# A planned mLSTM and mixture-of-experts kernel: its order found in rounds forward and backward, chunk 0's low halves from SBUF

## The chip, the cores and the metric

One core of a Trainium2 chip. The metric is the device time of the whole kernel in microseconds (us); the time before is the median of three runs.

## What is computed

Three layers, one after the other, all inputs in HBM.

An mLSTM over 4 batches, 8 heads, 768 steps, head width 40, with exponential gates and a running maximum m:

```python
m_new = np.maximum(f_gate[:, :, t] + m, i_gate[:, :, t])
C = f_stab[..., None, None] * C + i_stab[..., None, None] * np.einsum('bhd,bhe->bhde', vt, kt)
n = f_stab[..., None] * n + i_stab[..., None] * kt
denom = np.maximum(np.abs(nq), 1.0)                      # nq = n . q
y[:, :, t] = sigmoid(o_gate) * (C @ q) / denom
```

Its output, 3072 tokens of 320, goes through a dense layer, `h = x @ w_in` (320 x 2048), `g = h * sigmoid(h)`, `x = g @ w_out` (2048 x 320), and then through eight experts: each token goes to the one with the largest gate logit, `gate * relu(x @ w1[e]) @ w2[e]` with 1024 hidden columns. `w_in` and `w_out` come as float64, all else as float32.

## The kernel before, in words

The kernel multiplies in float16 with a high and a low part for each operand: a value is scaled, rounded to its high half, and the low half is the difference. So every product is three (or eight, with 320 = 128 + 128 + 64 rows) matmuls, and every value that feeds one needs a copy (the high half, ScalarE) and a subtraction (the low half, VectorE or GpSimd).

The mLSTM is done in 6 chunks of 128 steps for each of 4 batches: 24 units of 128 tokens (`unit(t)`, L568). Units 0 to 3 are chunk 0. A unit loads k, q, v and the output gate, splits them, turns K and Q (by TensorE for t < 3, by a transposing DMA on SP's queue from t = 3 on, L554 to L566), multiplies K by Q for the scores (L661), gates them (L663), takes high and low half (L667, L669), multiplies by V (L687 to L689), divides by the denominator (`denom`, L695 to L700: copy, absolute value by negation and maximum, maximum with 1 and scaling, reciprocal), takes halves of y and turns it into `xt`. Other than in the last chunk it also updates the batch's state (L724 to L749).

`l1(t, g)` (L902) multiplies tile t by a quarter of w_in (32 matmuls, L921), applies the tanh form of the gate (L923, L927) and takes halves (L930, L933). For t >= 4 and odd g the gated value lies in SBUF and GpSimd takes the low half; else it stays in PSUM and VectorE takes it, since GpSimd works from SBUF here. `l2(t, g)` (L940) multiplies by w_out (L953 to L955). Every four tiles `route` picks the experts and scatters the rows.

The float64 weights are narrowed to float32 by three integer instructions on VectorE (`narrow`, L760): L769 shifts the high word, L772 joins the sign, L775 joins the low word. For w_out (`conv_out`, L833) the middle value goes through `cvo_b`, 2560 bytes of PSUM that fill bank 3 and reach into bank 4. Bank 3 and bank 4 also hold the second layer's sums, in turns. Each converted block of w_out is turned by TensorE through one bank (`wt`, bank 2; L859, L860), copied (L862) and folded with the expert gate's weights (L872).

From the first expert on, 28 slots of 128 rows each (`slot`, L1139) multiply rows by an expert's weights; the weights come through two, later three staging buffers (`load_e`, L1076) and are split by ScalarE and VectorE (L1100 to L1115).

What sets the order: nothing is issued where it stands. Each `op(...)` adds a step to a plan with its engine (or two engines to choose from), a reckoned time, its dependencies and a `rank`, and, for loads, a time before which it may not start (`after`). `Plan.order` (L158) simulates the engines once: at each turn the engine that can start first takes the ready step with the lowest rank. The steps are then issued in the order of the simulated start times, each engine's queue in that order. The ranks come from the tile's position and from the table `RK` (L28). A step marked `port` is kept apart from GpSimd's steps in the simulation. The reckoned times are constants and lines such as

```python
def dve(n):
    return (n + 151) / 0.96
def pool2(n):
    return 100 + 2.25 * n
```

Of the kernel before, what the change touches and what calls it, by code (L numbers as in the profile page):

```python
# [27 lines left out]
RK = dict(  # L28
    tiles=20.71, win=4.19, dwin=3.47, wout=36.32, dwout=1.2, u0=-11.64, u1=12.12, u2=43.76, u3=-70.67,
    lead1=31.42, lead=30.5, l1c=-9.11, l2c=59.64, l2=21.72, gates=35.48, load=15.59, state=26.07, route=20.7,  # L30
)
# [7 lines left out]
def act(n):  # L39
    return 186 + 0.833 * n  # L40
# [6 lines left out]
def dve(n):  # L47
    return (n + 151) / 0.96
# [65 lines left out]
class Plan:  # L114
# [3 lines left out]


    HOP = 120  # L120
    DEEP = 5000
# [35 lines left out]

    def order(self):  # L158
        n = len(self.ops)
        need = [len(o[2]) for o in self.ops]  # L160
        after = [[] for _ in range(n)]
        for i, o in enumerate(self.ops):
            for d in o[2]:
                after[d].append(i)
        at = [max(0.0, o[6]) for o in self.ops]
        engines = ["PE", "ACT", "DVE", "POOL", "SP"]
        free = {e: 0.0 for e in engines}
        wait = {e: [] for e in engines}
        ready = {e: [] for e in engines}
        taken = [None] * n  # L170
        bus = port = begun = 0.0
        out = []

        def offer(i):
            for e in self.ops[i][0]:
                heapq.heappush(wait[e], (at[i], i))

        for i in range(n):
            if need[i] == 0:
                offer(i)  # L180
        while len(out) < n:
            best = None
            for e in engines:
                while ready[e] and taken[ready[e][0][1]]:
                    heapq.heappop(ready[e])
                while wait[e] and taken[wait[e][0][1]]:
                    heapq.heappop(wait[e])
                if ready[e]:
                    t = free[e]
                elif wait[e]:  # L190
                    t = max(free[e], wait[e][0][0])
                else:
                    continue
                if best is None or t < best[0]:
                    best = (t, e)
            t, e = best
            while wait[e] and wait[e][0][0] <= t:
                i = heapq.heappop(wait[e])[1]
                if not taken[i]:
                    heapq.heappush(ready[e], (self.ops[i][3], i))  # L200
# [21 lines left out]
            for j in after[i]:  # L222
# [4 lines left out]
        out.sort(key=lambda x: x[0])  # L227
        self.out = out
        return out

    def emit(self, engines):
# [6 lines left out]
def mlstm_moe_kernel(ctx, tc, q, k, v, ig, fg, og, w_in, w_out, w_gate, w1, w2, out):  # L238
# [20 lines left out]
    def op(*args, **kw):  # L259
        plan[0].op(*args, **kw)  # L260
# [8 lines left out]
    PS = Region(psp, "PS", 16384)  # L269
    groups = dict(l0=[0, 1], l1=[0, 1, 2], l2=[(4, 128), (3, 0)], at=[5, 6, 7], gt=[2], wt=[2], pg=[(2, 480)])  # L270
    turn = dict.fromkeys(groups, 0)
# [296 lines left out]
    def unit(t):  # L568
# [86 lines left out]
        for g in range(2):  # L655
            ps, kk = bank("at", 128, 4, CH)

            def scores(g=g, ps=ps):
                for j in range(4):
                    h = 4 * g + j  # L660
                    pe.matmul(ps[:, j, :], kT.ap[0:120, h, :], qT.ap[0:120, h, :], start=True, stop=True)  # L661
            op("PE", 4 * 60, scores, R=[kT, qT], W=[kk], rank=p + 6 + g)
            op("DVE", dve(512), lambda g=g, ps=ps: ve.scalar_tensor_tensor(  # L663
                out=ps, in0=ps, scalar=1.0 / SQ, in1=lam[g].ap, op0=ALU.mult, op1=ALU.mult
            ), R=[lam[g]], W=[kk], rank=p + 6 + g)
            P2 = P2_b[g]
            op("ACT", act(512), lambda P2=P2, ps=ps: ac.copy(out=P2.ap[:, 0], in_=ps),  # L667
               R=[kk], W=[P2], rank=p + 7 + g)
            op("DVE", dve(512), lambda P2=P2, ps=ps: ve.tensor_tensor(  # L669
                out=P2.ap[:, 1], in0=ps, in1=P2.ap[:, 0], op=ALU.subtract  # L670
            ), R=[kk], W=[P2], rank=p + 7 + g)
        if c > 0:
# [8 lines left out]
            ), R=[ki, "E"], W=[hb], rank=p + 8)  # L681
        pv, kv = bank("at", 128, H, D1)

# [11 lines left out]
        def denom():  # L695
            nq = pv[:, :, D:D1]
            ve.tensor_copy(out=den, in_=nq)
            ve.scalar_tensor_tensor(out=den, in0=den, scalar=-1.0, in1=nq, op0=ALU.mult, op1=ALU.max)
            ve.tensor_scalar(out=den, in0=den, scalar1=SQ * SQ, scalar2=2.0 / SY, op0=ALU.max, op1=ALU.mult)
            ve.reciprocal(out=den, in_=den)  # L700
        op("DVE", 640, denom, R=[kv], W=[kd], rank=p + 11)
        y = pv[:, :, 0:D]
# [54 lines left out]
    cv_b = [PS.cut([128, 512], F32, at=2048 * i) for i in (3, 4)]  # L757
    cvo_b = PS.cut([128, 640], F32, at=2048 * 3)

    def narrow(T, X, mid, z, n, rank):  # L760

        if not wide:
# [13 lines left out]
            out=o, in0=lo, scalar=29, in1=m, op0=ALU.logical_shift_right, op1=ALU.bitwise_or  # L776
        ), R=[T], W=[X, mid], rank=rank)

# [54 lines left out]
    def conv_out(f0):  # L833
# [7 lines left out]
        ), W=[T], rank=rk - 16, lag=2300, move=2100)  # L841
        narrow(T, X, cvo_b, X, 2 * DM, rk)
        pair = wo_b[f0:f0 + 2]
# [58 lines left out]
    def l1(t, g):  # L902
# [8 lines left out]
        for half in range(2):  # L911
# [12 lines left out]
           R=[kk], W=[th], rank=rk)  # L924
        pool_ = g in BY_POOL and t >= B
        z, kz = (th.ap, th) if pool_ else (ps, kk)
        op("DVE", dve(512), lambda: ve.scalar_tensor_tensor(  # L927
            out=z, in0=th.ap, scalar=1.0, in1=ps, op0=ALU.add, op1=ALU.mult
        ), R=[kk, th], W=[kz], rank=rk)
        op("ACT", act(512), lambda: ac.copy(out=G.ap[:, 0], in_=z), R=[kz], W=[G], rank=rk + 2)  # L930
        name, ns = ("POOL", pool2(512)) if pool_ else ("DVE", dve(512))
        m = po if pool_ else ve
        op(name, ns, lambda: m.tensor_tensor(out=G.ap[:, 1], in0=z, in1=G.ap[:, 0], op=ALU.subtract),  # L933
           R=[kz], W=[G], rank=rk + 2)

# [490 lines left out]
```

## Time and profile before

| | us |
|---|---|
| median of 3 runs (lowest to highest) | 691.66 (689.37 to 691.77) |
| the profiled execution, its time | 690.1 |
| its span, first to last instruction | 688.1 |
| busy: TensorE / VectorE / ScalarE / GpSimd | 624.6 / 530.8 / 412.9 / 237.2 |
| mean granted TensorE clock | 0.944 |
| read from and written to HBM | 71.64 MB, 11.78 MB |

In the rows PE is TensorE's matmuls, PEld its weight loads, DVE VectorE, ACT ScalarE, POOL GpSimd, SP the sync engine; SPq and the like are their queues. L921 is line 921 of the kernel before. Names after a line are the memory regions: PS is PSUM, A, W, X, RO and SG are regions of SBUF. Matmuls overlap each other, so a matmul's own duration is longer than the step from one to the next.

### The profile page before, as it was taken

To read this page: it belongs to the slowest core of one execution; us is meant where nothing else is said; L and a number is where in the kernel's file an instruction comes from. 1 tells how busy PE (TensorE), PEld (TensorE's weight loads), DVE (VectorE), ACT (ScalarE), POOL (GpSimd) and SP (SyncE) were. 2 spreads that over 40 slices of the span, in tenths; PEclk is the share of its full clock that TensorE was granted. 3 is DMA by queue.
4 is the path that set the end of the run, shared out by engine and by line. 5 is a ranking of instruction groups with operands and counts; after the bars stand their busy time and mean duration, and the time that the engine had idled before them with its cause. 6 is when DMAs were issued, how large, how long until landed. Compare 5 with 4: busy or idle time off the path is not lost.

```text
span 688.1 us, 21335 instructions
## 1 busy us (share of the span) xinstructions
PE 624.6 (91%) x8494; PEld 529.9 (77%) x8494; DVE 530.8 (77%) x1114; ACT 412.9 (60%) x832; POOL 237.2 (34%) x385
## 2 busy tenths in 40 slices
PE   4628779999999999999999999999979999979993
PEld 3517448898788888888888888887868888768882
DVE  6898678788998899998989989856848666756531
ACT  5754558768768787877777787544325444534320
POOL 3214113315455564538442532412302222313221
PEclk9667679999999999999999999999989999999997
DMA  8971864869978968867994975452479788867700
GB/s 191 233 162 25 190 153 95 211 148 210 197 171 144 169 137 157 159 138 163 147 152 88 187 131 122 124 109 84 126 170 234 222 222 202 218 183 186 165 8 25
DMA packets 254454, 105.96 MB, mean 154 GB/s; under 512 B 193381, under 2 KB 247976, under 8 KB 254344
## 3 DMA queue, kind: packets, MB, share of 16 engines
q1 hardware_dynamic: 251464, 95.82, 66.6%
q0 software_dynamic: 2880, 8.68, 3.5%
q8 instruction: 68, 1.11, 0.7%
q14 instruction: 42, 0.34, 0.2%
HBM read 71.64 MB, written 11.78 MB: 121 GB/s over the span
## 4 chain that ended last, share of the span: by engine, by line
PE 70%; DVE 12%; DMA 7%; ACT 3%; SPq 3%; issue 2%; POOL 0%; POOLq 0%; ACTq 0%; DVEq 0%
PE PS L921 25%; PE PS L953 8%; PE PS L954 8%; PE PS L955 8%; PE PS L1159 6%; DMA SG<-in_moe_w_dram 5%; PE PS L1172 2%; PE PS L1173 2%; PE PS L1174 2%; DMA X<-in_moe_w_dram 2%; PE PS L661 2%; DVE W L1163 1%; DVE A L1104 1%; DVE A L1115 1%; ACT A L1100 1%
## 5 line engine op out<-in xcount | busy, mean ns | idle before, releaser
L921 PE MATMUL PS<-A,A 128*128 128x128 f16 x3072 | 194.4, 221 | 3.0 <-ACT A L566 1.8
L921 PEld LDWEIGHTS <-A 128*128 128x128 f16 x3072 | 180.4, 99 | 8.5 <-issue 2.3
L1159 PE MATMUL PS<-W,A 128*128 128x128 f16 x1792 | 119.2, 222 | 10.5 <-DVE W L1163 10.5
L1159 PEld LDWEIGHTS <-A 128*128 128x128 f16 x1792 | 110.8, 99 | 19.3 <-issue 11.5
L955 PE MATMUL PS<-A,A 128*128 128x328 f16 x344 | 105.5, 307 | 0.0
L953 PE MATMUL PS<-A,A 128*128 128x328 f16 x344 | 105.4, 307 | 0.0
L954 PE MATMUL PS<-A,A 128*128 128x328 f16 x344 | 105.4, 306 | 0.0
L923 ACT ACTIVATE A<-PS 128x512 f32<-128x512 f32 x96 | 57.2, 596 | 54.0 <-PE PS L921 52.8
L1189 POOL DMA_INDIRECT out_dram<-W,sid x28 | 33.5, 1197 | 145.1 <-DVE W L1163 76.9
L933 POOL TENSOR_TENSOR A<-A 128x512 f16<-128x512 f32 x40 | 48.1, 1201 | 80.7 <-ACT A L930 75.9
L1174 PE MATMUL PS<-A,W 128*128 128x320 f16 x224 | 67.5, 301 | 0.9 <-DVE W L1163 0.9
L1172 PE MATMUL PS<-A,W 128*128 128x320 f16 x224 | 67.8, 303 | 0.0
L1173 PE MATMUL PS<-A,W 128*128 128x320 f16 x224 | 67.6, 302 | 0.0
L1163 DVE SCALAR_TENSOR_TENSOR W<-PS,W 128x512 f16<-128x512 f32 x56 | 38.0, 685 | 26.6 <-ACT W L1161 26.3
L616 ACT ACTIVATE A<-A,bias_t 128x128 f32<-128x128 f32 x160 | 58.0, 397 | 0.2 <-POOL A L594 0.2
L1161 ACT ACTIVATE W<-PS 128x512 f16<-128x512 f32 x56 | 32.4, 587 | 42.6 <-PE PS L1159 42.5
L927 DVE SCALAR_TENSOR_TENSOR PS<-A,PS 128x512 f32<-128x512 f32 x56 | 38.5, 688 | 15.3 <-ACT A L923 15.0
L1100 ACT ACTIVATE A<-SG 128x768 f16<-128x768 f32 x34 | 28.6, 841 | 33.9 <-DMA SG<-in_moe_w_dram 33.9
L955 PEld LDWEIGHTS <-A 128*128 128x128 f16 x344 | 34.0, 99 | 15.1 <-issue 0.3
L1104 DVE SCALAR_TENSOR_TENSOR A<-SG,A 128x512 f16<-128x512 f32 x34 | 25.5, 751 | 25.5 <-ACT A L1100 25.3
L953 PEld LDWEIGHTS <-A 128*128 128x128 f16 x344 | 33.9, 99 | 12.0
L954 PEld LDWEIGHTS <-A 128*128 128x128 f16 x344 | 34.0, 99 | 11.7
(247 smaller groups left out, 1353.6 us busy)
## 6 DMA issues: line engine op xcount, KB each, us to landing
SG<-in_moe_w_dram SPq DMA_DIRECT2D x34, 320.0 KB
A<-lam_d SPq DMA_DIRECT2D x40, 256.0 KB
SG<-in_moe_w_dram SPq DMA_DIRECT2D x34, 256.0 KB
A<-in_moe_w_out_dram SPq DMA_DIRECT2D x8, 640.0 KB
RO<-in_moe_w_dram SPq DMA_DIRECT2D x14, 320.0 KB
SG<-in_moe_w_dram SPq DMA_DIRECT2D x68, 64.0 KB
A<-in_moe_w_in_dram SPq DMA_DIRECT2D x8, 512.0 KB
A<-in_k_dram SPq DMA_DIRECT2D x24, 160.0 KB
```

What stands on the lines that cost most here:

```text
L616: ac.activation(out=lam[h // 4].ap[:, h % 4, :], in_=x, func=AF.Exp, bias=bias_t[:, c, b * H + h:b * H + h + 1])
L921: pe.matmul(ps[:, f, :], a, x, start=(n == 0), stop=(n == len(terms) - 1))
L923: op("ACT", act(512), lambda: ac.activation(out=th.ap, in_=ps, func=AF.Tanh, scale=0.5 * HS), R=[kk], W=[th], rank=rk)
L933: op(name, ns, lambda: m.tensor_tensor(out=G.ap[:, 1], in0=z, in1=G.ap[:, 0], op=ALU.subtract), R=[kz], W=[G], rank=rk + 2)
L953: pe.matmul(ps, gh, w[:, 0, :], start=(f == 0), stop=False)
L954: pe.matmul(ps, gh, w[:, 1, :], start=False, stop=False)
L955: pe.matmul(ps, gl, w[:, 0, :], start=False, stop=(f == NF - 1))
L1159: pe.matmul(ps[:, jj, :], l, m, start=(n == 0), stop=(n == len(terms) - 1))
L1163: op("DVE", dve(512), lambda hh=hh, ps=ps: ve.scalar_tensor_tensor(out=hh.ap[:, 1], in0=ps, scalar=0.0, in1=hh.ap[:, 0], op0=ALU.max, op1= ...
L1172: pe.matmul(ps, hh[:, 0, f % 4, :], x[:, 0, :], start=(f == 0), stop=False)
L1173: pe.matmul(ps, hh[:, 0, f % 4, :], x[:, 1, :], start=False, stop=False)
L1174: pe.matmul(ps, hh[:, 1, f % 4, :], x[:, 0, :], start=False, stop=(f == NF2 - 1))
```

## The change

Five things.

1. `Plan.order` no longer simulates once. It runs eight rounds: forward as before, with the given ranks; then `backward` goes through the same steps from the end, on the engines that the forward round chose, and the time by which each step has to start becomes its rank for the next round. The round with the earliest simulated end is kept. So `RK` gives only the first round's ranks, and the `after` times. `RK` is new.
2. In chunk 0 the gated scores are written over `lam` in SBUF and not back to PSUM, and the low half may be taken by VectorE or GpSimd, whichever the plan finds free. The same for the gated values of tiles 0 to 3 in `l1`.
3. w_out's middle value stays in its SBUF buffer X; `cvo_b` is gone.
4. w_out's transposes take turns in banks 2 and 3.
5. The denominator takes three instructions: the sign bit is masked off into eight spare columns of the same PSUM bank, then maximum and scaling, then the reciprocal.

```diff
-    tiles=20.71, win=4.19, dwin=3.47, wout=36.32, dwout=1.2, u0=-11.64, u1=12.12, u2=43.76, u3=-70.67,
-    lead1=31.42, lead=30.5, l1c=-9.11, l2c=59.64, l2=21.72, gates=35.48, load=15.59, state=26.07, route=20.7,
+    tiles=19.85, win=0.74, dwin=24.63, wout=-131.33, dwout=-7.89, u0=26.52, u1=35.48, u2=-170.13, u3=-317.32,
+    lead1=167.42, lead=30.23, l1c=-161.68, l2c=189.66, l2=41.51, gates=165.41, load=70.38, state=-103.43, route=-150.74,
...
+    def backward(self, out):
...
+        for _ in range(n):
+            t, e = self.step(free, wait, ready)
+            while wait[e] and wait[e][0][0] <= t:
+                i = heapq.heappop(wait[e])[1]
+                heapq.heappush(ready[e], (-last[i], i))
+            i = heapq.heappop(ready[e])[1]
+            end = free[e] = t + self.ops[i][0][e]
+            late[i] = -end / 1e3
+            for d in self.ops[i][2]:
+                lag, move = self.ops[d][4:6]
+                at[d] = max(at[d], end + self.HOP + lag + (move if lag else 0.0))
...
+    def order(self):
...
+        rank = [o[3] for o in self.ops]
+        best = None
+        for _ in range(self.ROUNDS):
+            out = self.forward(rank)
+            end = max(x[1] for x in out)
+            if best is None or end < best[0]:
+                best = end, out
+            rank = self.backward(out)
...
-    groups = dict(l0=[0, 1], l1=[0, 1, 2], l2=[(4, 128), (3, 0)], at=[5, 6, 7], gt=[2], wt=[2], pg=[(2, 480)])
+    groups = dict(l0=[0, 1], l1=[0, 1, 2], l2=[(4, 128), (3, 0)], at=[5, 6, 7], gt=[2], wt=[2, 3], pg=[(2, 480)])
...
+            z, kz = (lam[g].ap, lam[g]) if c == 0 else (ps, kk)
+            op("DVE", dve(512), lambda g=g, ps=ps, z=z: ve.scalar_tensor_tensor(
+                out=z, in0=ps, scalar=1.0 / SQ, in1=lam[g].ap, op0=ALU.mult, op1=ALU.mult
+            ), R=[kk, lam[g]], W=[kz], rank=p + 6 + g)
...
+            flex = c == 0
+            op(DP if flex else "DVE", dp(512) if flex else dve(512), lambda m=ve, P2=P2, z=z: m.tensor_tensor(
+                out=P2.ap[:, 1], in0=z, in1=P2.ap[:, 0], op=ALU.subtract
+            ), R=[kz], W=[P2], rank=p + 7 + g, port=flex)
...
-            ve.tensor_copy(out=den, in_=nq)
-            ve.scalar_tensor_tensor(out=den, in0=den, scalar=-1.0, in1=nq, op0=ALU.mult, op1=ALU.max)
-            ve.tensor_scalar(out=den, in0=den, scalar1=SQ * SQ, scalar2=2.0 / SY, op0=ALU.max, op1=ALU.mult)
-            ve.reciprocal(out=den, in_=den)
-        op("DVE", 640, denom, R=[kv], W=[kd], rank=p + 11)
+            ve.tensor_scalar(
+                out=dn.bitcast(I32), in0=nq.bitcast(I32), scalar1=0x7FFFFFFF, scalar2=None, op0=ALU.bitwise_and
+            )
+            ve.tensor_scalar(out=dn, in0=dn, scalar1=SQ * SQ, scalar2=2.0 / SY, op0=ALU.max, op1=ALU.mult)
+            ve.reciprocal(out=den, in_=dn)
+        op("DVE", 540, denom, R=[kv], W=[kd], rank=p + 11)
...
-    cvo_b = PS.cut([128, 640], F32, at=2048 * 3)
...
-        ), R=[T], W=[X, mid], rank=rank)
+        ), R=[T], W=[X, mid], rank=rank, port=mid is X)
...
-        narrow(T, X, cvo_b, X, 2 * DM, rk)
+        narrow(T, X, X, X, 2 * DM, rk)
...
-        pool_ = g in BY_POOL and t >= B
-        z, kz = (th.ap, th) if pool_ else (ps, kk)
+        pool_, flex = g in BY_POOL and t >= B, t < B
+        z, kz = (th.ap, th) if pool_ or flex else (ps, kk)
...
+        name, ns = (DP, dp(512)) if flex else ("POOL", pool2(512)) if pool_ else ("DVE", dve(512))
```

## Rows read from the trace of the kernel before

**Rows 1.** The page, its second part: 40 equal slices of the span.

```profile
PE   4628779999999999999999999999979999979993
...
DVE  6898678788998899998989989856848666756531
...
PEclk9667679999999999999999999999989999999997
```

**Rows 2.** Busy time by stretch: PE, PEld, DVE, ACT, POOL, granted clock, DMA share, GB/s.

```profile
0.00:105.30 105.30, 64.94 (x712) 49.18 (x713) 84.08 (x170) 61.46 (x116) 25.78 (x63) 0.72 0.71 160
105.30:463.00 357.70, 357.46 (x5277) 308.02 (x5275) 315.20 (x693) 263.14 (x581) 156.74 (x232) 1.00 0.76 151
463.00:500.00 37.00, 35.95 (x443) 30.16 (x441) 28.78 (x85) 14.16 (x24) 11.33 (x18) 1.00 0.36 106
500.00:520.00 20.00, 15.61 (x186) 13.62 (x184) 9.54 (x16) 7.48 (x12) 1.82 (x5) 0.83 0.78 188
...
580.00:620.00 40.00, 34.03 (x430) 29.15 (x429) 24.31 (x41) 17.72 (x27) 9.01 (x13) 0.98 0.76 202
```

**Rows 3.** Waits of VectorE and TensorE until 106 us: total, times, longest.

```profile
DVE A L775 <- PE PS L955: 3.5, 1, 3.5
DVE PS L927 <- ACT A L923: 3.0, 3, 1.2
DVE PS L772 <- PE PS L955: 2.9, 1, 2.9
DVE W L471 <- DMA W<-in_i_gate_dram: 2.8, 1, 2.8
...
DVE A L801 <- ACT A L799: 1.6, 1, 1.6
...
PE PS L689 <- DVE A L669: 4.6, 3, 2.7
```

**Rows 4.** VectorE's groups until 105.3 us, by shape: busy us, mean ns; idle before.

```profile
L769 DVE TENSOR_SCALAR A<-A 128x640 int32<-128x640 int32 x8 | 5.1, 647 | 0.0
...
L933 DVE TENSOR_TENSOR A<-PS,A 128x512 f16<-128x512 f32 x6 | 4.1, 678 | 0.0
L669 DVE TENSOR_TENSOR A<-PS,A 128x512 f16<-128x512 f32 x6 | 4.0, 678 | 0.0
L603 DVE SCALAR_TENSOR_TENSOR A<-A 128x320 f16<-128x320 f32 x5 | 3.1, 627 | 0.1
...
L610 DVE SCALAR_TENSOR_TENSOR A<-A 128x320 f16<-128x320 f32 x5 | 2.4, 480 | 0.0
...
L699 DVE TENSOR_SCALAR den<-den 128x8 f32<-128x8 f32 x3 | 1.0, 336 | 0.1
```

**Rows 5.** Timeline of VectorE, GpSimd and TensorE: start and duration in us.

```profile
16.14 1.28 DVE L669 TENSOR_TENSOR A<-PS,A 128x512 f16<-128x512 f32 x2
...
54.99 2.20 DVE L769 TENSOR_SCALAR A<-A 128x640 int32<-128x640 int32 x2
...
55.15 1.70 POOL L475 TENSOR_TENSOR W<-W 32x640 f32<-32x640 f32 x1 [3.23 <-DVE W L471]
...
65.04 2.85 PE L921 MATMUL PS<-A,A 128*128 128x128 f16 x48
...
78.60 0.48 DVE L769 TENSOR_SCALAR A<-A 128x640 int32<-128x640 int32 x1
```

**Rows 6.** Groups of the whole span by shape: busy us, mean ns; idle before.

```profile
L923 ACT ACTIVATE A<-PS 128x512 f32<-128x512 f32 x96 | 57.2, 596 | 54.0 <-PE PS L921 52.8 <-PE PS L1012 0.4 <-POOL A L594 0.4
...
L933 POOL TENSOR_TENSOR A<-A 128x512 f16<-128x512 f32 x40 | 48.1, 1201 | 80.7 <-ACT A L930 75.9 <-issue 4.7
...
L698 DVE SCALAR_TENSOR_TENSOR den<-den,PS 128x8 f32<-128x8 f32 x24 | 3.9, 162 | 0.8
```

**Rows 7.** Waits of SP's queue and of ScalarE, whole span.

```profile
SPq L556 <- DVE A L714: 26.3, 12, 4.9
...
ACT A L1100 <- DMA X<-in_moe_w_dram: 23.3, 10, 6.9
```

More of the change, by code (lines that the diff above doesn't have):

```diff
@@ L156, in op, with step, forward @@
                          -1e9 if after is None else 1e3 * after, port))
-    def order(self):
+    ENGINES = ("PE", "ACT", "DVE", "POOL", "SP")
+    ROUNDS = 8
+    def step(self, free, wait, ready, taken=()):
+        best = None
+        for e in self.ENGINES:
+            for x in (ready[e], wait[e]):
+                while taken and x and taken[x[0][1]]:
+                    heapq.heappop(x)
+            if ready[e]:
+                t = free[e]
+            elif wait[e]:
+                t = max(free[e], wait[e][0][0])
+            else:
+                continue
+            if best is None or t < best[0]:
+                best = (t, e)
+        return best
+    def forward(self, rank):
         n = len(self.ops)
         need = [len(o[2]) for o in self.ops]
[L161 to L164, printed above, removed]
         at = [max(0.0, o[6]) for o in self.ops]
[L166 to L169, printed above, removed]
+        free = {e: 0.0 for e in self.ENGINES}
+        wait = {e: [] for e in self.ENGINES}
+        ready = {e: [] for e in self.ENGINES}
         taken = [None] * n
@@ L181, in order @@
         while len(out) < n:
[L182 to L196, printed above, removed]
+            t, e = self.step(free, wait, ready, taken)
             while wait[e] and wait[e][0][0] <= t:
@@ L199, in order @@
                 if not taken[i]:
-                    heapq.heappush(ready[e], (self.ops[i][3], i))
+                    heapq.heappush(ready[e], (rank[i], i))
             i = heapq.heappop(ready[e])[1]
@@ L221, in order @@
             out.append((t, end, i, e))
-            for j in after[i]:
+            for j in self.after[i]:
                 at[j] = max(at[j], end + self.HOP)
@@ L226, in order @@
                     offer(j)
-        out.sort(key=lambda x: x[0])
-        self.out = out
-        return out
+        return out
+    def backward(self, out):
+        n = len(self.ops)
+        on = [None] * n
+        last = [0.0] * n
+        for t, _, i, e in out:
+            on[i], last[i] = e, t + self.ops[i][0][e]
+        need = [len(x) for x in self.after]
+        at = [0.0] * n
+        free = {e: 0.0 for e in self.ENGINES}
+        wait = {e: [] for e in self.ENGINES}
+        ready = {e: [] for e in self.ENGINES}
+        late = [0.0] * n
+        for i in range(n):
+            if need[i] == 0:
+                heapq.heappush(wait[on[i]], (0.0, i))
+        for _ in range(n):
[9 more added lines that the diff above has]
+                at[d] = max(at[d], end + self.HOP + lag + (move if lag else 0.0))
+                need[d] -= 1
+                if need[d] == 0:
+                    heapq.heappush(wait[on[d]], (at[d], d))
+        return late
+    def order(self):
+        n = len(self.ops)
+        self.after = [[] for _ in range(n)]
+        for i, o in enumerate(self.ops):
+            for d in o[2]:
+                self.after[d].append(i)
+        rank = [o[3] for o in self.ops]
+        best = None
+        for _ in range(self.ROUNDS):
[4 more added lines that the diff above has]
+            rank = self.backward(out)
+        self.out = sorted(best[1], key=lambda x: x[0])
+        return self.out
     def emit(self, engines):
@@ L662, in unit @@
             op("PE", 4 * 60, scores, R=[kT, qT], W=[kk], rank=p + 6 + g)
-            op("DVE", dve(512), lambda g=g, ps=ps: ve.scalar_tensor_tensor(
-                out=ps, in0=ps, scalar=1.0 / SQ, in1=lam[g].ap, op0=ALU.mult, op1=ALU.mult
-            ), R=[lam[g]], W=[kk], rank=p + 6 + g)
+            z, kz = (lam[g].ap, lam[g]) if c == 0 else (ps, kk)
+            op("DVE", dve(512), lambda g=g, ps=ps, z=z: ve.scalar_tensor_tensor(
+                out=z, in0=ps, scalar=1.0 / SQ, in1=lam[g].ap, op0=ALU.mult, op1=ALU.mult
+            ), R=[kk, lam[g]], W=[kz], rank=p + 6 + g)
             P2 = P2_b[g]
[L667 to L671, printed above, removed]
+            op("ACT", act(512), lambda P2=P2, z=z: ac.copy(out=P2.ap[:, 0], in_=z),
+               R=[kz], W=[P2], rank=p + 7 + g)
+            flex = c == 0
+            op(DP if flex else "DVE", dp(512) if flex else dve(512), lambda m=ve, P2=P2, z=z: m.tensor_tensor(
+                out=P2.ap[:, 1], in0=z, in1=P2.ap[:, 0], op=ALU.subtract
+            ), R=[kz], W=[P2], rank=p + 7 + g, port=flex)
         if c > 0:
@@ L681, in unit @@
             ), R=[ki, "E"], W=[hb], rank=p + 8)
-        pv, kv = bank("at", 128, H, D1)
+        pv, kv = bank("at", 128, H * D1 + H)
+        dn = pv[:, H * D1:].unsqueeze(2)
+        pv = pv[:, 0:H * D1].rearrange("p (h d) -> p h d", d=D1)
         def values():
@@ L930, in l1 @@
         op("ACT", act(512), lambda: ac.copy(out=G.ap[:, 0], in_=z), R=[kz], W=[G], rank=rk + 2)
[L931 to L934, printed above, removed]
+        name, ns = (DP, dp(512)) if flex else ("POOL", pool2(512)) if pool_ else ("DVE", dve(512))
+        m_ = po if pool_ else ve
+        op(name, ns, lambda m=m_: m.tensor_tensor(out=G.ap[:, 1], in0=z, in1=G.ap[:, 0], op=ALU.subtract),
+           R=[kz], W=[G], rank=rk + 2, port=flex)
     yb = {}
```

## The prediction

> **What bounds the kernel now.** I read the slices first. The reader is to see three stages [rows 1]: six slices of some 17 us in which TensorE stands at 2 to 8 tenths while VectorE has 6 to 9; a long middle with TensorE at 9; and an end with two dents. The table of stretches puts numbers to them [rows 2]. Until 105.3 us TensorE is busy 64.9 us, at a mean granted clock of 0.72, so part of that at the lower of its two levels (1.2 GHz), and VectorE is busy 84.1. From 105.3 to 463 TensorE is busy 357.46 of 357.70 us at full clock: this stretch is TensorE's alone, and nothing on another engine is worth anything in it. In the expert stage it idles 4.4 us in 500 to 520 and 6.0 us in 580 to 620.
>
> From this follows the rule of my sum. The change adds and removes no matmul, so the middle stays as long as it is; what can move the end is how early TensorE becomes full (now 105.3 us), and how much it idles behind 463. Until 105.3 the work that holds it up is VectorE's: splitting chunk 0's values, converting both float64 weights, the low halves of the gated values. So I cost the start on VectorE and take each microsecond that VectorE loses there as one off the end.
>
> Third, the waits before 106 us [rows 3]. Two are VectorE waiting for a second-layer matmul (L955) in the PSUM bank that the w_out conversion uses: 3.5 and 2.9 us. Two more (L927 and L801 waiting for ScalarE) are 3.0 and 1.6 us: VectorE's next instruction was not ready and it issues in order. TensorE's own waits there, such as 4.6 us of L689 for a score half, are the mirror of VectorE being behind.
>
> **The change part by part.**
>
> *Low halves to GpSimd.* Before 105.3 us VectorE does six of the score halves (L669) and six of the gate halves (L933), 678 ns each [rows 4]; back to back two of them take 1.28 us, 0.64 each [rows 5]. If the planner sends these twelve to GpSimd, VectorE loses 12 x 0.64 = 7.7 us. The other two and ten fall behind 105.3, where VectorE is not the bound: nothing. GpSimd takes 1201 ns for one [rows 6]; 12 x 1.2 = 14.4 us beside the 25.8 of 105.3 that it is busy now [rows 2], so it has room. Behind such a half on GpSimd's queue stand the weighted values, the state's low part and the copy that completes y (L645, L649, L742, L712); each can come up to 1.2 us later, and TensorE and the transposing DMAs wait for them. A score half itself is 0.52 us longer on GpSimd: six are 3.1 us more for TensorE's L689, which already waits 4.6 us for them [rows 3]. TensorE has 40 us of idle time there, which hides it; without this cover it would cost the 3.1. That z of chunk 0 now lies in SBUF frees its bank after the gating instruction. For the gates it is held in one of two buffers through tanh (0.6 [rows 6]), gate (0.64), copy (taken like the tanh) and half (1.2), 3.0 us, so 1.5 us per group; the 32 matmuls of a group take 1.9 at full clock, two thirds of the 2.85 for 48 [rows 5]: no new bound.
>
> *w_out in SBUF.* The 3.5 and 2.9 us of waiting for L955 go [rows 3]: 6.4 us. Late next is the load or the copy behind each block. The second transposing bank takes waits from TensorE alone, which is not the bound here: nothing. Bank 3 is still shared with every second tile's second layer and with the w_in conversion, which can bring a wait back; the term lies between 0 and 6.4, and I take 6.4, since the row names the very bank that is given up.
>
> *Shorter denominators.* One instruction of 162 ns goes (L698 [rows 6]), and L699, 336 ns on average until 105.3 [rows 4], works from PSUM; it takes 0.17 when nothing disturbs it, as its neighbour L698 does. So 0.33 for each of three units: 1.0 us. The other units lie in the full stretch: nothing.
>
> *Contention, given back.* VectorE is slowed where GpSimd runs: two L769 took 2.20 us across a GpSimd addition that began at 55.15, one alone takes 0.48 [rows 5]. Over the stretch the excess is 8 x (0.647 - 0.48) = 1.3 for L769, 5 x (0.627 - 0.48) = 0.7 for L603 against its twin L610, 3 x 0.17 = 0.5 for L699 [rows 4]: 2.5 us for 25.8 us of GpSimd, 0.1 per microsecond. For 14.4 us more that is 1.4. The w_out chain now reads SBUF alone in one more step, so I take 2. Bounds: 0, if the planner, which keeps such instructions apart, is right; 14.4, if VectorE stands still through every one.
>
> The Trainium skill (SBUF — State Buffer, Who interferes with whom) speaks for that upper end: a VectorE instruction with two SBUF inputs and a GpSimd instruction that reads SBUF exclude each other, and the later one blocks for the whole of the other. The trace agrees in kind, by the 2.20 us; by the page alone the sum would lose those 14.4 us and not 2.
>
> *The order.* Every instruction, load and transposing DMA gets a new place, on SP's and GpSimd's queues too, and no row shows it. Gain: L927 and L801 waited 4.6 us with other work left to do [rows 3]; a priority by latest start should fill that. More is open: VectorE's idle time until 105.3 is 21.2 us, less 6.4 and 4.6, less the 2.8 before its first data [rows 3], leaves some 7; behind 463 there are 10.4 us [rows 2], whose waits are for weights [rows 7]. Loss: the full stretch has no slack at all, so any wait put there lengthens the run. I take 4.6, the row nearest, and keep both ends.
>
> **Sum.** 7.7 + 6.4 + 1.0 + 4.6 - 2.0 = 17.7 us. The profiled execution took 690.1 us (688.1 of span): 672.4. The median shown is 691.66, 1.6 above it; so for the median 674.0. A measurement of this kernel can tell about 0.5%, 3.5 us, from no change: 688.2 and 695.1 are the marks.
>
> **The rivals.**
>
> A. *The order helps more than I count.* The last waits behind 463 go as well, and the remaining VectorE idle time: 17.7 + 7 + 10.4 = 35: 656.6, and up to 665 for part of it. For it: the waits for weights (23.3 us for X alone [rows 7]) fall where the transfer engines are 0.36 busy just before, in 463 to 500 [rows 2], so loads could come earlier. Against: the loads have not-before times and two or three staging buffers, neither changed.
>
> B. *Contention takes the gain.* By the rule above every GpSimd half blocks VectorE for its 1.2 us: 17.7 - 12.4 = 5.3 left, 686; and without the order's gain 691. Against it: the rows give 0.1 per microsecond and not 1, and the planner, now told of the second step of the w_out chain, spaces them.
>
> C. *Slower: the new order stalls TensorE in the full stretch.* 20 units (t = 4 to 23) go through it, each with transposes on SP's queue, which already wait 26.3 us in twelve times for L714 [rows 7] without TensorE noticing. An order that puts the steps of a unit just ahead of their need leaves TensorE, which issues in order, standing where the chip is later than planned. It decides from 17.7 / 20 = 0.9 us a unit; at 1.5 us the run takes 691.7 - 17.7 + 30 = 704. Against it: the planner reckons 691 ns for a 512-wide VectorE instruction, where the rows give steps of 0.64, and 1252 for a GpSimd half that takes 1201, so work is mostly ready earlier than planned. For it: its transfers are constants.
>
> D. *The flexible halves stay on VectorE.* The planner gives each to whichever engine is free first. Then 7.7 - 2.0 are missing: 680. This lies within my forecast's range.
>
> **How the numbers follow.** Forecast with D: 0.49, 665 to 686 (the contention up to half of its bound; the bank's 6.4 lost). A: 0.19, 650 to 665. B: 0.14, 686 to 692. C: 0.18, 692 to 715. Faster by over 0.5% (under 688.2): 0.49 + 0.19 + 0.04 of B = 0.72. Slower (over 695.1): 0.16 of C. The rest, 0.12, is the same. The range of 8 in 10 leaves out the far half of A and the far half of C: 657 to 700.
>
> **What would show it.** In the new profile: L933 and L669 stand on GpSimd at about 1.2 us for most of 24; no VectorE wait for L955 ahead of L772 or L775; TensorE full from about 88 to 92 us and not 105.3; the stretch of 358 us that follows as full as now. If TensorE becomes full as early as that and the end does not move, C is right and the middle holds new waits. If VectorE's instructions with two SBUF inputs grow to 1 us and more and TensorE becomes full as late as now, B is. If the middle is as full and the stretch from the first expert to the end shrinks, A is. I would be wrong altogether if TensorE filled later than at 105 us.

## The result, and the profile after

The changed kernel takes 674.56 us (median of 4 runs, 672.25 to 674.92); the kernel before, beside it, 690.52. The ratio (of the means) is 0.9761, with a 95% interval of 0.973 to 0.9793: faster by 2.4%. The forecast was 674.0. The profiled execution took 674.64 us, with a span of 672.9, against 690.1 and 688.1.

First the page's second part of the changed kernel, the span in 40 slices, to be held beside [rows 1].

```profile
PE   2356999999999999999999999999999999979892
...
DVE  7998688778879899899899878857848667646630
...
PEclk9996999999999999999999999999999999989997
```

TensorE reaches its nines in the fifth slice and not in the seventh, and has fewer dents near the end. VectorE's row is no emptier. The table of stretches says how much (busy time of PE, PEld, DVE, ACT, POOL, granted clock, DMA share, GB/s), for the stretches of [rows 2] and a few others:

```profile
0.00:70.00 70.00, 32.78 (x366) 27.50 (x367) 59.17 (x116) 40.81 (x74) 28.84 (x60) 0.90 0.72 191
70.00:105.30 35.30, 35.11 (x537) 28.02 (x535) 28.49 (x49) 27.75 (x58) 12.34 (x12) 1.00 0.55 109
0.00:105.30 105.30, 67.89 (x900) 55.52 (x901) 87.66 (x164) 68.56 (x131) 41.18 (x72) 0.94 0.66 163
...
105.30:459.20 353.90, 353.90 (x5162) 304.68 (x5160) 300.32 (x657) 257.54 (x571) 162.67 (x237) 1.00 0.76 151
```

The same cut of the kernel before, and two short stretches of it that are used further down:

```profile
0.00:70.00 70.00, 36.55 (x435) 30.99 (x435) 58.07 (x122) 41.26 (x77) 19.47 (x55) 0.76 0.66 151
70.00:105.30 35.30, 28.39 (x277) 18.19 (x278) 26.01 (x49) 20.20 (x40) 6.30 (x8) 0.66 0.81 179
105.30:459.20 353.90, 353.66 (x5237) 304.98 (x5235) 313.27 (x689) 261.26 (x578) 156.74 (x232) 1.00 0.77 151
...
80.00:85.00 5.00, 5.00 (x27) 2.66 (x27) 0.85 (x3) 1.11 (x2) 0.66 (x2) 0.50 0.94 258
95.00:100.00 5.00, 4.96 (x27) 2.70 (x27) 1.47 (x4) 2.11 (x5) 0.24 (x1) 0.54 0.50 145
```

Until 70 us TensorE does less than before; from 70 us on it is full, at full clock, where the kernel before has 28.4 busy of 35.3 us at 0.66. So by 105.3 us it has issued 900 instructions and not 712. In the full stretch before, 5237 instructions take 353.66 us, 0.068 us each: the 188 more are an estimate of 12.7 us of work that need not be done later. Yet TensorE was busy only 3.0 us longer by then (67.89 against 64.94), so most of this is speed: the 28.39 us before, at 0.66, are worth an estimated 18.7 at full clock, and the 35.11 after are at full clock. VectorE's busy time until 105.3 did not fall, it rose, from 84.1 to 87.7.

Where the end moved is read from one line's first and last matmul: the second layer (L955, now L1009) and the experts' first product (L1159, now L1213). Columns: times it ran, shortest, median and longest in ns, first and last start. Before:

```profile
L955 PE MATMUL PS<-A,A x344: 301/303/481, 81.8 to 471.3; 128*128 128x328 f16 x172
...
L1159 PE MATMUL PS<-W,A x1792: 216/219/315, 463.7 to 670.7; 128*128 128x128 f16 x200
```

After:

```profile
L1009 PE MATMUL PS<-A,A x344: 301/302/303, 90.5 to 459.2; 128*128 128x328 f16 x172
...
L1213 PE MATMUL PS<-W,A x1792: 216/219/314, 454.2 to 654.5; 128*128 128x128 f16 x200
```

The first stage ends 12.1 us earlier (471.3 to 459.2). From there to the last matmul of the experts' first layer it is 199.4 us before and 195.3 after: 4.1 more. The 17.7 of the sum came out nearly right in size (688.1 - 672.9 = 15.2 of span, with about 1 us given back behind that last matmul), but a quarter of it lies where the prediction counted nothing, and the experiments show that most of its terms were not what paid.

The waits until 106 us, after (total, times, longest), against [rows 3]:

```profile
DVE A L937 <- PE PS L914: 3.6, 1, 3.6
DVE A L823 <- DMA A<-in_moe_w_out_dram: 3.2, 1, 3.2
DVE A L855 <- ACT A L853: 2.8, 1, 2.8
...
PE PS L614 <- DVE A L653: 10.6, 1, 10.6
PE PS L779 <- DVE A L714: 7.5, 1, 7.5
```

VectorE's waits for the second layer's bank are gone, and others of the same size stand there. TensorE's two longest waits for VectorE are longer than the 4.6 us of [rows 3]; both lie ahead of 70 us, and no run shows what they cost.

And the groups of VectorE and GpSimd until 105.3 us, by shape (busy us, mean ns; idle before), where the moved halves are L721 and L987:

```profile
L823 DVE TENSOR_SCALAR A<-A 128x512 int32<-128x512 int32 x10 | 7.2, 731 | 0.0
...
L521 DVE TENSOR_TENSOR_SCAN W<-W 32x640 f32<-32x640 f32 x1 | 2.4, 2436 | 0.0
...
L721 DVE TENSOR_TENSOR A<-A 128x512 f16<-128x512 f32 x2 | 1.9, 966 | 0.0
...
L721 POOL TENSOR_TENSOR A<-A 128x512 f16<-128x512 f32 x6 | 8.8, 1473 | 19.8 <-ACT A L718 19.8
L987 POOL TENSOR_TENSOR A<-A 128x512 f16<-128x512 f32 x3 | 3.6, 1201 | 5.3 <-ACT A L984 5.3
...
L987 POOL TENSOR_TENSOR A<-A,A 128x512 f16<-128x512 f32 x2 | 2.5, 1240 | 4.0 <-ACT A L984 4.0
...
L987 POOL TENSOR_TENSOR SG<-A,SG 128x512 f16<-128x512 f32 x1 | 1.3, 1296 | 0.8 <-ACT SG L984 0.8
```

Twelve halves until 105.3 on GpSimd, as the prediction counted (18 of 24 in all). They take 16.2 us there, and other instructions of VectorE are slow: the first step of w_in's conversion averages 731 ns, against 478 before.

### The profile page after: what moved, and what is told of

Same layout as the page of the kernel before. It is cut to its first block, busy times and chain, and to the rows that moved or that the text cites. A ratio compares the mean times of both kernels' runs of the same rounds, so it can differ in the third digit from the quotient of the medians.

```text
span 672.9 us, 21314 instructions
## 1 busy us (share of the span) xinstructions
PE 615.8 (92%) x8494; PEld 526.2 (78%) x8494; DVE 518.7 (77%) x1074; ACT 412.6 (61%) x835; POOL 252.8 (38%) x398
## 4 chain that ended last, share of the span: by engine, by line
PE 81%; DVE 7%; DMA 6%; SPq 2%; ACT 1%; issue 1%; POOL 0%; POOLq 0%; ACTq 0%; DVEq 0%
PE PS L975 26%; PE PS L1213 11%; PE PS L1007 8%; PE PS L1008 8%; PE PS L1009 8%; PE PS L1226 3%; PE PS L1227 3%; PE PS L1228 3%; DMA SG<-in_moe_w_dram 3%; PE PS L711 2%; DMA A<-in_moe_w_out_dram 1%; DMA X<-in_moe_w_dram 1%; PE PS L913 1%; PE PS L741 1%; PE PS L779 1%
## 5 line engine op out<-in xcount | busy, mean ns | idle before, releaser
L975 PE MATMUL PS<-A,A 128*128 128x128 f16 x3072 | 192.1, 221 | 2.9 <-DVE A L855 2.9
L1213 PE MATMUL PS<-W,A 128*128 128x128 f16 x1792 | 118.1, 221 | 7.2 <-DVE W L1217 6.7
L1213 PEld LDWEIGHTS <-A 128*128 128x128 f16 x1792 | 109.7, 99 | 16.3 <-issue 7.6
L1007 PE MATMUL PS<-A,A 128*128 128x328 f16 x344 | 104.0, 302 | 0.0
L1009 PE MATMUL PS<-A,A 128*128 128x328 f16 x344 | 104.0, 302 | 0.0
L1008 PE MATMUL PS<-A,A 128*128 128x328 f16 x344 | 104.0, 302 | 0.0
L987 POOL TENSOR_TENSOR A<-A 128x512 f16<-128x512 f32 x43 | 51.5, 1197 | 95.5 <-ACT A L984 93.0
L1243 POOL DMA_INDIRECT out_dram<-W,sid x28 | 31.0, 1106 | 146.7 <-DVE W L1231 66.9
L666 ACT ACTIVATE A<-A,bias_t 128x128 f32<-128x128 f32 x160 | 56.4, 397 | 0.0
L1215 ACT ACTIVATE W<-PS 128x512 f16<-128x512 f32 x56 | 32.4, 586 | 39.0 <-PE PS L1213 27.6
L981 DVE SCALAR_TENSOR_TENSOR A<-A,PS 128x512 f32<-128x512 f32 x56 | 38.0, 679 | 10.1 <-ACT A L977 10.0
L1009 PEld LDWEIGHTS <-A 128*128 128x128 f16 x344 | 33.6, 98 | 14.3
L1158 DVE SCALAR_TENSOR_TENSOR A<-SG,A 128x512 f16<-128x512 f32 x34 | 25.4, 746 | 23.5 <-ACT A L1154 23.3
```

The lines of the kernel that those rows point to most:

```text
L666: ac.activation(out=lam[h // 4].ap[:, h % 4, :], in_=x, func=AF.Exp, bias=bias_t[:, c, b * H + h:b * H + h + 1])
L975: pe.matmul(ps[:, f, :], a, x, start=(n == 0), stop=(n == len(terms) - 1))
L987: op(name, ns, lambda m=m_: m.tensor_tensor(out=G.ap[:, 1], in0=z, in1=G.ap[:, 0], op=ALU.subtract), R=[kz], W=[G], rank=rk + 2, port=flex)
L1007: pe.matmul(ps, gh, w[:, 0, :], start=(f == 0), stop=False)
L1008: pe.matmul(ps, gh, w[:, 1, :], start=False, stop=False)
L1009: pe.matmul(ps, gl, w[:, 0, :], start=False, stop=(f == NF - 1))
```

## The experiments

All against the kernel before on the same chip, where that took 693 to 694 us (690.52 beside the change itself); so ratios are compared, not times. Diffs are against the kernel after unless they say otherwise. The columns of this table: the ratio with its interval; TensorE's instructions until 105.3 us; its granted clock from 70 to 105.3 us; the start of the last second-layer matmul; from there to the start of the last matmul of the experts' first layer. The runs whose order was not found in rounds are marked with a star.

```
run                        ratio  interval         PE until 105.3   clock 70-105   last 2nd layer   experts
before *                   1                       712              0.66           471.3            199.4
after                      0.9761 0.973  - 0.9793  900              1.00           459.2            195.3
e1_order_only              0.9934 0.9906 - 0.9963  761              0.75           471.5            196.5
e2_parts_only *            0.9979 0.995  - 1.0008  705              0.65           474.6            198.6
e3_halves_on_vector        0.9752 0.969  - 0.9814  892              1.00           460.5            191.9
e4_wout_psum               0.9894 0.9858 - 0.9931  783              0.85           471.6            195.8
e5_gates_psum              0.9881 0.9829 - 0.9933  692              0.86           470.5            190.7
e6_one_bank                0.9964 0.9927 - 1.0001  684              0.76           476.0            195.3
e7_wout_mid_psum           0.9811 0.9757 - 0.9866  914              1.00           465.2            194.6
e8_three_rounds            0.9926 0.9897 - 0.9954  695              0.84           474.9            194.4
e9_fill_before *           1.0056 1.0022 - 1.0091  650              0.71           480.5            200.0
e10_wout_sbuf_before *     1.0004 0.9979 - 1.0028  710              0.61           473.7            197.9
e11_order_and_wout         0.9762 0.971  - 0.9814  849              1.00           462.5            194.2
e12_six_rounds             0.9844 0.9777 - 0.991   813              0.95           463.0            195.7
```

(For e9 the 380 added idle matmuls are taken off.)

Two things in the table hold for all runs. The last two columns come from one profile each: after, e3 and e11 have the same order of steps and differ by 3.3 us in the end of the second layer and by 3.4 in the experts' stretch. And the clock from 70 us on sorts the ends of the second layer: the five runs at 0.95 to 1.00 end it at 459.2 to 465.2, the nine at 0.61 to 0.86 at 470.5 to 480.5.

**The change cut in two: the order alone, and the data paths alone.**

```diff
-            z, kz = (lam[g].ap, lam[g]) if c == 0 else (ps, kk)
-            flex = c == 0
+            z, kz = ps, kk
+            flex = False
...
-        narrow(T, X, X, X, 2 * DM, rk)
+        narrow(T, X, cvo_b, X, 2 * DM, rk)
...
-        pool_, flex = g in BY_POOL and t >= B, t < B
+        pool_, flex = g in BY_POOL and t >= B, False
```

(with one bank for the transposes and the old denominators as well: e1). The other half has all the data paths, one round and the old table:

```diff
-    ROUNDS = 8
+    ROUNDS = 1
```

> The order in eight rounds and the new table, with all data paths as before (scores and gates back to PSUM with the halves on VectorE, w_out through PSUM, one transposing bank, four denominator instructions). Theory of the prediction (VectorE's work at the start is the price, the order is worth 4.6 us): about 686 us. Rival (the order does it, the parts are worth little by themselves): 675 to 679 us, TensorE full by about 85 us, and the expert stage as short as in the changed kernel.

> All changed data paths, but one pass of the planner with the table of before. Theory of the prediction: the parts are worth 7.7 + 6.4 + 1.0 - 2.0 = 13.1 us, so about 677 us. Rival (the order does it): 688 us or more, no better than before, because ranks set for the old durations place the moved halves badly.

The order alone gives 0.7%, 4.6 us of 693.6, just the term; but its second layer ends where it ended before, and what the profile shows of the gain lies with the experts (199.4 to 196.5). The data paths alone give nothing that can be measured: the rival's case. 4.6 and 1.5 are far from the 16.6 of the whole (2.39% of 693): as drawn here, the parts of the change do not add up.

**The halves given back to VectorE, the order untouched.** Only the engine that issues the 18 halves differs.

```diff
-            op(DP if flex else "DVE", dp(512) if flex else dve(512), lambda m=ve, P2=P2, z=z: m.tensor_tensor(
+            op(DP if flex else "DVE", dp(512) if flex else dve(512), lambda m=ve, P2=P2, z=z: ve.tensor_tensor(
...
-        op(name, ns, lambda m=m_: m.tensor_tensor(out=G.ap[:, 1], in0=z, in1=G.ap[:, 0], op=ALU.subtract),
+        op(name, ns, lambda m=m_: (ve if flex else m).tensor_tensor(out=G.ap[:, 1], in0=z, in1=G.ap[:, 0], op=ALU.subtract),
```

> The changed kernel with its order untouched on every engine, but the 18 halves that the plan gave to GpSimd are issued on VectorE at their place in time. Theory of the prediction: twelve of them before 105 us cost VectorE 7.7 us and save it the contention, so 678 to 682 us. Rival (contention takes the relief back): within 1 us of the changed kernel's 674.6, and the two-input instructions of VectorE at their quiet durations.

The time is that of the change, as far as its interval tells (up to 0.9814, 0.5% above the change): the rival's case. Without the 5.7 us that the prediction counted for the halves (7.7 less 2.0) it would be 0.984. Its stretch until 105.3 us, and three of VectorE's groups in it:

```profile
0.00:105.30 105.30, 67.81 (x892) 55.36 (x893) 89.24 (x175) 68.11 (x130) 26.03 (x60) 0.94 0.68 161
...
L721 DVE TENSOR_TENSOR A<-A 128x512 f16<-128x512 f32 x8 | 5.9, 735 | 0.8 <-ACT A L718 0.8
L823 DVE TENSOR_SCALAR A<-A 128x512 int32<-128x512 int32 x10 | 4.3, 440 | 0.2 <-DMA A<-in_moe_w_in_dram 0.2
...
L521 DVE TENSOR_TENSOR_SCAN W<-W 32x640 f32<-32x640 f32 x1 | 1.5, 1532 | 0.0
```

VectorE has twelve more halves here, 11.2 us for fifteen against 3.0 for three in the kernel after, so 8.2 us of work; its busy time is higher by only 89.24 - 87.66 = 1.6. The other 6.6 had been given back to slowed instructions: 2.9 in L823 alone, 0.9 in the scan L521. The 1.6 us don't show in the time: TensorE is full from 70 us in both.

**One data path back at a time, order found anew.** In e4 w_out goes through PSUM again and the transposes have one bank; in e5 chunk 0's gated values go back to PSUM and their halves to VectorE; in e6 only the second transposing bank is taken away; in e7 only w_out's middle value goes back.

```diff
-        narrow(T, X, X, X, 2 * DM, rk)
+        narrow(T, X, cvo_b, X, 2 * DM, rk)
...
-    groups = dict(l0=[0, 1], l1=[0, 1, 2], l2=[(4, 128), (3, 0)], at=[5, 6, 7], gt=[2], wt=[2, 3], pg=[(2, 480)])
+    groups = dict(l0=[0, 1], l1=[0, 1, 2], l2=[(4, 128), (3, 0)], at=[5, 6, 7], gt=[2], wt=[2], pg=[(2, 480)])
```

(both lines are e4, the first alone e7, the second alone e6; e5 takes the three z, flex and pool_ lines of e1.)

> The changed kernel with w_out converted through PSUM and its transposes in one bank again; the planner orders anew. Theory of the prediction: the 6.4 us of waits for L1009 in that bank come back, about 681 us, with VectorE waiting for it ahead of L826 or L829. Rival (the rounds order around the bank): 674 to 677 us and no such wait of over 1 us.

> The changed kernel with the gated scores and gates of chunk 0 back in PSUM and their low halves on VectorE; w_out, banks, denominators and rounds as changed; the planner orders anew. Theory after the first four runs (the first stage's 12 us come from the w_out edits and the rounds together, the halves are worth nothing): 674 to 678 us, last matmul of the second layer near 460 us. Rival (holding the gated values in SBUF frees PSUM banks, and this is the part that the order needs): 682 to 688 us, last second-layer matmul near 470.

> The changed kernel with w_out's transposes in bank 2 alone; all else as changed, ordered anew. If the second bank is what the w_out edits bring: 682 to 686 us and TensorE waiting several us for the copies L916. If the conversion in SBUF is it: 674 to 678 us.

> The changed kernel with w_out's middle value through PSUM banks 3 and 4 again, the transposes in two banks; ordered anew. If the conversion in SBUF is what the w_out edits bring: 682 to 686 us. If the second bank is it: 674 to 678 us.

Taken as they stand, they say that each of the parts is worth 3 to 14 us of 693, the most for the bank to which the prediction gave nothing (e7's 3 lie within its interval). The waits came back in part: until 106 us VectorE waits 2.5 us for the second layer in e4, where 6.4 were expected, and TensorE 4.7 us for the copies in e6. e5 came out as its rival says, in time and in the end of the second layer. But the four numbers cannot be the parts' worth, since the order is found anew each time and differs everywhere. The next run shows how much that alone is.

**All the parts, but the best of the first three rounds, or of six.**

```diff
-    ROUNDS = 8
+    ROUNDS = 3
```

(e12: ROUNDS = 6.)

> The changed kernel with the best of the first three rounds and not of eight: no part differs, only the order drawn. If the order drawn is worth little beside the parts: within 3 us of 674.6. If the last rounds matter, or a drawn order is a matter of luck of several us: 679 us or more, which would also say how much of the single-part runs is the draw.

> The kernel after with six drawn rounds instead of eight, so that the best of the first six orders is used; all data paths stay. If the data paths carry the gain, an order that the planner ranks almost as high gives 673 to 677 (ratio 0.973 to 0.980). If the gain hangs on the one order that was drawn, it lies between the run with three rounds (688.3) and the change: 679 to 687 (ratio 0.983 to 0.993).

Nothing but the order differs, and it costs 11 us with three rounds and 6 with six (0.9926 and 0.9844 less 0.9761, of 693). So which of the PSUM edits is worth what can't be read from e4 to e7. The stretch until 105.3 and the two longest waits of TensorE in e8:

```profile
0.00:105.30 105.30, 57.90 (x695) 46.02 (x696) 83.79 (x158) 59.75 (x109) 32.37 (x67) 0.90 0.62 154
...
PE PS L779 <- DVE A L714: 12.4, 1, 12.4
PE PS L614 <- ACT A L766: 12.1, 2, 6.8
```

TensorE stands 47 of 105 us, against 37 in the kernel after, where these waits are 7.5 and 3.9. The column "PE until 105.3" goes with the end of the second layer (at 0.068 us an instruction, counted from the kernel before) to within 3 us in most runs; e1, e4 and e9 end 3.5 to 5 us later than that, and e7, with 914 and an end at 465.2, nearly 8. e7 idles 2.9 us between 105.3 and 459.2, which is part of that.

**The clock alone.** The kernel before, its order untouched, with idle matmuls in TensorE's planned pauses. Diff against the kernel before:

```diff
+    def filler(ap):
+        for _ in range(plan[0].fill):
+            pe.matmul(ap, ident16, ident16, start=True, stop=True)
```

> The kernel before, its order untouched, with some 390 idle 128x128 matmuls put into TensorE's planned pauses of the first 105 us; their results are written over by the group that follows. No work of VectorE or GpSimd changes. If the clock of the start carries the first stage (TensorE's work of 65 us there ran at a mean granted clock of 0.72 before and 0.94 after), the granted clock of the first 105 us rises from 0.72 to above 0.82, TensorE is full before 100 us, and the time falls to 678 to 686 (ratio 0.980 to 0.992). If VectorE's work holds TensorE up there, as the prediction's rule has it, the clock rises all the same but the time stays at 688 to 696 (ratio 0.995 to 1.006), with TensorE full from 105 us as before.

Stretches of this run:

```profile
0.00:105.30 105.30, 78.56 (x1030) 67.03 (x1032) 80.36 (x162) 56.36 (x107) 22.11 (x59) 0.84 0.65 149
0.00:70.00 70.00, 49.20 (x713) 46.09 (x716) 55.47 (x115) 37.68 (x70) 18.06 (x54) 0.90 0.65 150
```

The column until 70 us now reads what it reads in the kernel after (0.90), and the time is 0.6% worse. So a higher clock until 70 us does not shorten this order. The test is blunt at one side, since the added matmuls also stand ahead of real ones (the first w_in matmul comes at 32.4 and not at 27.0). And it says nothing of the stretch behind 70 us, where the clock rose only from 0.66 to 0.71 and the kernel after has 1.00: there, by the rows of the result, lies most of what TensorE gained, and no run raises the clock there with the order of before held.

**w_out through SBUF, in the order of before.** Diff against the kernel before:

```diff
-        a, m, o = X.ap.bitcast(I32), mid.ap.bitcast(I32), z.ap.bitcast(I32)
+        a, m, o = X.ap.bitcast(I32), (X if mid is cvo_b else mid).ap.bitcast(I32), z.ap.bitcast(I32)
```

> The kernel before, its order untouched, with one edit: the middle value of w_out's conversion is kept in SBUF and not in PSUM, so the two-bank PSUM tile of L955 is no longer written or read by it. The prediction's term: the VectorE waits for L955 ahead of L772 (2.9 us) and L775 (3.5 us) go, and come off the end: 684 (ratio about 0.991). The rival, after the run of all data paths in the old order gave nothing: the waits go, others take their place, 689 to 692 (ratio 0.996 to 1.002).

Nothing at all, within 0.3%: the rival's case. Two of VectorE's waits between 80 and 112 us there:

```profile
DVE A L862 <- PE PS L860: 4.5, 2, 2.3
...
DVE A L883 <- ACT A L607: 2.2, 1, 2.2
```

No wait for L955 is left; VectorE waits instead for the transposes (4.5 us in L862, where the kernel before has 0.3). Its busy time from 70 to 105.3 is 26.4 us, against 26.0.

**The order with the PSUM edits only.** From the kernel after, the halves on VectorE (as in e3) and the four-instruction denominators, the order untouched.

> The kernel after, its order untouched, with the 18 low halves issued on VectorE and the old four-instruction denominators: only the drawn order and w_out's way through SBUF are left of the change. If the order carries the gain and the data paths only make that order possible, 674 to 677 (ratio 0.974 to 0.981). If the shorter denominators and the halves each bring what the prediction gave them (1.0 and 7.7), 680 to 684 (ratio 0.984 to 0.991).

The expectation leaves out two things that also stay in this run: the gated values of chunk 0 in SBUF, and the second transposing bank. So what is taken away is all that relieves VectorE of work, and what stays is the order and all that frees PSUM. The ratio is that of the whole change, 0.9762, with an interval of 0.5% to either side. Together with e2 and e8, which have all the parts and other orders, this shows what carries the gain: the order that was drawn, on these data paths.

## Why the prediction was right, and where it was not

**The size and the range: right, the size by luck. The rule under the sum: wrong.** "Each microsecond that VectorE loses there" taken "as one off the end" fails both ways. 8.2 us of halves given back to VectorE cost nothing that the interval tells (e3), and the waits taken from it bring nothing (e10). The terms behind 17.7 were not what paid, so that the median came within 0.6 us of the forecast is chance. The first stage ends early where TensorE has much behind it by 105.3 us, and the order sets that: VectorE is busy no less until then (87.7 against 84.1). That it depends on which of VectorE's work comes first is argued, not shown; the granted clock from 70 us on (0.66 before, 1.00 after) goes with it, as cause or as consequence.

**Low halves to GpSimd, 7.7: nothing shown.** The count (12) and the engine were as said; a gate half took 1.20 to 1.30 us, about the 1.2 of the sum, a score half 1.47. 6.6 of the 8.2 us came back as contention, where the prediction took 2.0, and the rest cannot be seen in the time while the order holds. The estimate of 0.1 us per microsecond of GpSimd was drawn from other GpSimd work; here it is 6.6 / 16.2 = 0.4. Rival B was nearer on this term, though not on the time. Rival D, the halves left on VectorE, was priced at 680; e3 is that case, with the order held, and is as fast as the change.

**Contention, 2.0: three times that.** Single instructions are held for the whole of a GpSimd step and more. In VectorE's and GpSimd's timeline of the kernel after (start and duration), one L823 takes 2.65 us across two GpSimd steps, where the ten of e3 average 0.44:

```profile
82.13 2.65 DVE L823 TENSOR_SCALAR A<-A 128x512 int32<-128x512 int32 x1
...
82.17 1.15 POOL L987 TENSOR_TENSOR A<-A 128x512 f16<-128x512 f32 x1
83.28 1.22 POOL L644 TENSOR_SCALAR_AFFINE_SELECT A<-A 128x512 f32<-128x512 f32 x2
```

The rule of the Trainium skill (SBUF — State Buffer, Who interferes with whom), by which the later of two such instructions is blocked for the whole of the other, would have given back all of the GpSimd time, 16.2 us. The trace agrees for single instructions in how long one is held, by the 2.65 us, and not for the sum, 6.6. It does not show that the later one is blocked: this L823 starts 0.04 us ahead of the half. Nor are the rows of the pair that the prediction named, two inputs in SBUF: L823 here, and L769 in [rows 5], each read one.

**w_out in SBUF, 6.4: no gain by itself.** The two waits went, as predicted, and were replaced (e10). They were not VectorE's own delay: they end at 84.7 and 98.6 us, and from 80 to 85 and 95 to 100 us TensorE is busy 5.00 and 4.96 of 5 us at a granted clock of 0.50 and 0.54 (the two short rows in the result). There VectorE waited for TensorE at its lower level, which the prediction's "until 105.3 the work that holds it up is VectorE's" leaves out. What the change does with it is another thing. The conversion's second step, first and last start, before and after:

```profile
L772 DVE SCALAR_TENSOR_TENSOR PS<-A x18: 672/700/1298, 11.7 to 110.0; 128x512 int32<-128x512 int32 x10, 128x640 int32<-128x640 int32 x8
```

```profile
L826 DVE SCALAR_TENSOR_TENSOR A<-A x8: 812/822/827, 5.6 to 91.3; 128x640 int32<-128x640 int32 x8
```

Before, the eight w_out blocks (640 wide) begin at 63.6 us and the last at 110; after, the first is at 5.6 and the last at 91.3. TensorE starts its last transpose of w_out at 101.6 us and not at 125.7. In every order found in rounds with w_out in SBUF this step of the first block starts before 6 us; in the three with it in PSUM (e1, e4, e7) at 57.7 to 60.4. An early w_out is not enough (e6, e8: 0.996 and 0.993) and not needed for all of the gain (e7: 0.981), so it is a trait of the order that won, not shown to be its cause.

**Denominators, 1.0: less work, no time seen.** Three instructions of 168, 174 and 207 ns until 105.3, where there were four; e11 has the old ones, and the halves on VectorE, and takes as long within 0.5%. That is 3.5 us, so a gain of 1.0 is neither shown nor excluded.

**The order, 4.6: the right size at the wrong place.** Alone it gives 4.6 us, of which the profiles show 2.9 with the experts and none before them. The ten runs with an order found in rounds have an expert stage of 190.7 to 196.5 us, 194.4 in the mean, and the four of the old kind 197.9 to 200.0, 199.0 in the mean. That is the stretch of rival A, which the prediction held apart at 0.19, with some 4 of its 10.4 us. TensorE's wait for an expert's first layer, before and then after:

```profile
PE PS L1159 <- DVE W L1163: 10.5, 5, 4.4
```

```profile
PE PS L1213 <- DVE W L1217: 6.7, 4, 3.1
```

A's mechanism, weights that come earlier, is not shown: ScalarE's wait for the weights in X was 23.3 us [rows 7] and is, after:

```profile
ACT A L1154 <- DMA X<-in_moe_w_dram: 25.9, 11, 5.2
```

In the first stage the order alone gives nothing, and the data paths alone give nothing; together 12 us. No term of the sum was for that. Terms of a sum are added as if each stood alone; in these runs the PSUM edits were worth something only to an order that uses the room (e2 and e11), and the order found without the room was worth little there (e1). The second half rests on one drawn order: that none without these edits is as good is not shown.

**Rival C: no.** From 105.3 to 459.2 TensorE is busy 353.90 of 353.90 us. TensorE was to be full from about 88 to 92 us on; it is from 70.

**What stays open:** which of the three PSUM edits (w_out's middle value, the second bank, the gated values in SBUF) the good order needs. It would take many orders of each variant and their mean, and that was not tried. Open too: whether the clock from 70 us on brings part of the gain or only follows from TensorE's work coming without pauses. How good the order is that is kept is in part luck: the best of three rounds gives 0.9926, of six 0.9844, of eight 0.9761.

## What to carry to other kernels

Before crediting a part of a change, hold the order of issue and undo the part alone: here the two edits that take work off the engine that looked like the bound turned out to be worth nothing that 0.5% tells, and only so was it seen. Where a program finds the order, every edit also draws a new order, whose spread (11 us here) can be larger than the edit's worth; an ablation that lets it find the order again measures both. And an engine that is busy 80% of a stretch is not yet its bound: ask which of its work the next engine is waiting for, whether room in PSUM would let that come first, and at which clock the other engine runs while it keeps this one waiting.

## What the runs showed that was not expected

The column of the granted clock cannot be trusted at the start of a run. In the kernel after it reads 1.00 in the first 40 us, with TensorE busy 11.9 us of them, and also from 35 to 43 us. But the 14 first-layer matmuls until 43 us take 311 ns each, against 221 in the whole run. In the kernel before the same matmul (L921) takes 309 ns from 24 to 30 us, where the column reads 0.50 from 20 us on, and 219 from 60 to 70 us, where it reads 1.00. So these ran at the lower level. The stretch, and the two groups:

```profile
35.00:43.00 8.00, 4.21 (x36) 3.69 (x37) 7.93 (x16) 4.86 (x8) 3.06 (x4) 1.00 0.98 208
...
L975 PE MATMUL PS<-A,A 128*128 128x128 f16 x14 | 1.7, 311 | 0.0
...
L975 PE MATMUL PS<-A,A 128*128 128x128 f16 x3072 | 192.1, 221 | 2.9 <-DVE A L855 2.9
```

Means that begin at 0 (0.72 before, 0.94 after, 0.84 in e9) are therefore too high, the prediction's too; those from 70 us on are not touched by it. A higher clock until 70 us is not worth time by itself (e9). GpSimd's own halves suffer as VectorE's instructions do: six score halves average 1473 ns, three gate halves beside them 1201.
